# Expert tiles of 512 tokens, one written order for five engines, and a state product in two halves

## The chip, the cores and the metric

One core of a Trainium2 chip. The metric is the device time of the whole program in microseconds. The kernel before took 532.48 us (median of three runs, 531.59 to 532.96). One more execution was profiled; every duration below is from that one.

## What is computed

Three layers, one after the other, all in float32:

```python
# 1. gated linear attention, 4 x 8 heads, 768 positions, head size 32, state 16
y = (CB * L) @ x + (C @ state) * decay          # per chunk
state = decay_full * state + B^T @ (x * decay)
# 2. x: 3072 tokens x 256
h = x @ w_in                                    # 256 -> 2048
x = maximum(0.01 * h, h) @ w_out                # 2048 -> 256
# 3. one expert of 8 for each token
logits = x @ w_gate + modality_bias[modality_id]
e = argmax(logits, axis=1)
out[e == k] = gate_w * (maximum(x[e == k] @ w1[k], 0) @ w2[k])   # 256 -> 1024 -> 256
```

## The kernel before, in words

**Attention and the dense layer.** The 3072 tokens are 24 chunks of 128, six chunks to a batch, and six blocks of 512. A chunk's `p3_mm` (line 584) makes its output and the addition to the state; from the second chunk of a batch on it begins with the state product, one matmul of `st` (128 rows) with `cdt` (256 columns: the transposed decayed C twice, each masked to one half of the heads by `cdt_evict`, line 547, two ScalarE operations). Its PSUM tile `psy` is one bank of `psa`. `cb_mm` (line 559) multiplies in four row groups of 32, into four banks, two of them of `pscb`. The dense layer is float32 in three float32r products: each operand is a high part and a rest (high x high, high x rest, rest x high). For each of 96 steps (block j, f) `h_mm` (line 712) issues six matmuls of 512 columns and `mm2` (line 752) six more. VectorE and ScalarE make the activation's high part `gh` and rest `gl` in between (lines 724 to 745).

**Routing.** After each block the logits, the one-hot choice and the rank of each token in its expert's list are worked out (`logits`, `ranks`; lines 784 to 905); `ranks_put` (line 894) scatters the token numbers into the list `il` in DRAM with four indirect DMAs from GpSimd, and `rows_out` (line 926) writes the block's rows to `yx` in DRAM.

**Experts.** A tile is T = 256 entries of an expert's list. `m2_idx` (line 1010) reads the list (`gi`, which waits for all the scatters so far) and gathers the rows of `yx` by two indirect DMAs, `m2_w` (line 998) loads the expert's weights, `m2_split1` and `m2_split2` (lines 1028, 1037) split them into high part and rest (the last quarter on GpSimd, the others on VectorE), `m2_xT` (line 1043) transposes the rows, `m2_mm1` (line 1056) issues 48 matmuls of 256 columns into four PSUM tiles (`psh`, `pscb`), `m2_mm2` (line 1075) 48 more into one accumulator for each group of 128 tokens; then the result is scaled (ScalarE) and scattered (GpSimd). Five tiles are chosen by a table made after block 3 (`table_early`), seven more by a table made at the end (`table_final`); up to seven more stand in conditional code (`cond`, line 1258). 3072 tokens are twelve full tiles.

**What sets the order.** To the end of block 4, `PLAN` (line 26) is the written order of PE, VectorE, ScalarE and GpSimd: each token is a step and its numbers, and each engine executes its instructions in the order of the tokens (line 1182). Block 5 and the experts are scheduled by the framework, with some steps pinned (`Q["pin"]`, lines 1198 to 1255). There the first tile's first product is spread over block 5; at the block's end come the logits, the ranks, the second tile's first half, and the table. SyncE's queue (SP: loads, `gi`, `yx`) is ordered by the framework throughout.

Of the kernel before, what the change touches and what calls it, by code (L numbers as in the profile page):

```python
# [45 lines left out]
    mul.6.1 y.9 or.o.3.0 sa.12 lb.o.3.1 p3.6 gg.11 gh.10 or.o.3.1 gh.11 h.13 load.10 xa.6 cast.o.3.0 gl.10 trmm.7
    exp.7.1 st.6 trd.7 y.10 gg.12 subg.o.3.0 xb.6 trb.7 trde.7 trc.7 h.14 gl.11 gh.12 bs.7 sa.13 gl.12 exp.8.0 cb.7
    gg.13 y.11 mul.7.3 sa.14 mul.7.2 mul.7.0 exp.8.1 mul.7.1 mask.9 y.12 gg.14 gh.13 bt cast.o.3.1 h.15 gh.14 gl.13
    exp.9.1 p3.7 cd.8 subv.o.3.1 sa.15 gl.14 trmm.8 load.11 xa.7 trd.8 y.13 trb.8 gg.15 trde.8 trc.8 exp.9.0 xb.7 y.14
    cd.9 bs.8 st.7 gh.15 bs.9 gl.15 h.16 cb.8 sa.16 cd.10 mask.10 h.17 gg.16 mul.8.2 gh.16 mul.8.3 h.18 exp.10.0  # L50
    mul.8.1 mul.8.0 gl.16 sa.17 p3.8 sa.18 gg.17 exp.10.1 gg.18 trmm.9 load.12 y.15 st.8 trb.9 xa.8 trc.9 bs.10 trd.9
    evV.0 evA.0 h.19 trde.9 xb.8 gh.17 lg.0 sa.19 gl.17 y.16 lt.0 gg.19 l2.0 gh.18 h.20 r1.0 mask.11 r2.0 rx.0 cb.9
    sa.20 gl.18 exp.11.0 y.17 mul.9.0 mul.9.1 mul.9.2 exp.11.1 mul.9.3 rp.0 r3.0 trmm.10 be.0 trd.10 trb.10 y.18
    trde.10 gh.19 trc.10 put.0 gg.20 p3.9 gl.19 gh.20 cd.11 yr.0.0 st.9 xa.9 load.13 h.21 yc.0.0 xb.9 gl.20 bs.11
    yr.0.1 sa.21 y.19 yc.0.1 gg.21 mask.12 ro.0 cb.10 gh.21 exp.12.0 h.22 mul.10.3 mul.10.0 mul.10.2 exp.12.1 mul.10.1
    trmm.11 gl.21 p3.10 trc.11 sa.22 h.23 trb.11 load.14 gg.22 xa.10 xb.10 st.10 y.20 sa.23 bs.12 gg.23 h.24 gh.22
    gl.22 y.21 sa.24 gg.24 h.25 gh.23 gl.23 trd.11 sa.25 y.22 trde.11 gg.25 cb.11 cd.13 gh.24 mask.13 y.23 mul.11.1
    mul.11.3 exp.13.1 mul.11.2 mul.11.0 h.26 gl.24 gh.25 exp.13.0 gl.25 p3.11 sa.26 y.24 bs.13 load.15 xa.11 gg.26
    xb.11 h.27 gh.26 gl.26 y.25 cd.14 sa.27 mask.14 gg.27 h.28 gh.27 exp.14.0 gl.27 y.26 sa.28 exp.14.1 gg.28 y.27
    gh.28 h.29 gl.28 h.30 sa.29 gg.29 y.28 sa.30 gh.29 gg.30 h.31 gl.29 gh.30 gl.30 y.29 sa.31 gg.31 trmm.12 gh.31  # L60
    h.32 trc.12 mask.15 trb.12 gl.31 cb.12 sa.32 exp.15.0 y.30 gg.32 mul.12.2 mul.12.1 exp.15.1 h.33 mul.12.0 mul.12.3
    gh.32 p3.12 sa.33 gl.32 gg.33 trmm.13 xa.12 load.16 y.31 trc.13 trb.13 xb.12 st.12 bs.14 h.34 evV.1 evA.1 gh.33
# [98 lines left out]
def kernel(  # L161
# [1143 lines left out]
```

## Time and profile before

| | |
|---|---|
| median of three runs | 532.48 us |
| the profiled execution, its own time | 531.67 us |
| its span, first to last instruction | 530.0 us |
| mean granted clock of TensorE | 0.984 |
| PE / VectorE / ScalarE / GpSimd busy | 95% / 66% / 60% / 29% |

A PE row's own duration counts a matmul from issue to its drained result, so rows of successive matmuls overlap; what one costs is the distance to the next one's start, or a row of the chain of waits divided by its count. All helpers record through one line (L225), so groups are told apart by the names of their tiles: `h` and `y` are the dense layer's products, `hp` and `o` the experts' first and second, `psy`, `ps` and `cb` attention's, `lp`, `l`, `rp` and `yr` the routing's, `xps` the transposes of a tile's rows `xg`.

### The profile page before, as it was taken

To read this page: it belongs to the slowest core of one execution; us is meant where nothing else is said; L and a number is where in the kernel's file an instruction comes from. 1 tells how busy PE (TensorE), PEld (TensorE's weight loads), DVE (VectorE), ACT (ScalarE), POOL (GpSimd) and SP (SyncE) were. 2 spreads that over 40 slices of the span, in tenths; PEclk is the share of its full clock that TensorE was granted. 3 is DMA by queue.
4 is the path that set the end of the run, shared out by engine and by line. 5 is a ranking of instruction groups with operands and counts; after the bars stand their busy time and mean duration, and the time that the engine had idled before them with its cause. 6 is when DMAs were issued, how large, how long until landed. Compare 5 with 4: busy or idle time off the path is not lost.

```text
span 530.0 us, 9745 instructions
## 1 busy us (share of the span) xinstructions
PE 501.8 (95%) x3520; PEld 411.9 (78%) x3520; DVE 347.4 (66%) x737; ACT 317.4 (60%) x667; POOL 154.5 (29%) x143
## 2 busy tenths in 40 slices
PE   7879999999999999999999999999899999999990
PEld 4546767777876787778777787878799999999990
DVE  5898999775576656775677655674875555566620
ACT  5859989674764656456644544543566666666630
POOL 5343223040100310041011260220435655655340
PEclk8999999999999999999999999999999999999996
DMA  8899934529543251494001850090467777767300
GB/s 196 151 218 217 268 61 94 87 21 89 102 71 70 39 103 22 84 77 101 1 1 24 268 172 1 22 92 9 135 85 219 238 227 235 230 204 228 101 24 23
DMA packets 128315, 61.05 MB, mean 115 GB/s; under 512 B 84546, under 2 KB 120515, under 8 KB 128259
## 3 DMA queue, kind: packets, MB, share of 16 engines
q1 hardware_dynamic: 125186, 53.94, 48.1%
q0 software_dynamic: 3072, 6.41, 3.8%
q8 instruction: 30, 0.49, 0.5%
q14 instruction: 27, 0.21, 0.1%
HBM read 53.73 MB, written 6.60 MB: 114 GB/s over the span
## 4 chain that ended last, share of the span: by engine, by line
PE 78%; DVE 7%; ACT 6%; issue 4%; DMA 2%; POOL 1%; POOLq 0%; DVEq 0%; ACTq 0%
PE y L225 22%; PE h L225 22%; PE hp L225 12%; PE o L225 10%; PE psy L225 3%; PE cb L225 2%; DVE hb L225 2%; PE ps L225 1%; PE yr L225 1%; DMA raw<-in_moe_w_out_dram 1%; ACT e L225 1%; DVE gl L225 1%; PE xps L225 1%; PE lp L225 1%; ACT hb L225 1%
## 5 line engine op out<-in xcount | busy, mean ns | idle before, releaser
L225 ACT ACTIVATE sa<-h 128x512 f32<-128x512 f32 x96 | 56.8, 596 | 67.5 <-PE h L225 63.9
L225 DVE TENSOR_TENSOR gg<-sa,h 128x512 f32<-128x512 f32 x96 | 65.4, 684 | 46.8 <-ACT sa L225 46.1
L225 DVE TENSOR_TENSOR gl<-gg,gh 128x512 fp32r<-128x512 f32 x96 | 69.7, 728 | 23.4 <-ACT gh L225 22.0
L225 PE MATMUL h<-xh,wih 128*128 128x512 f32 x192 | 78.7, 410 | 1.9 <-DVE gg L225 1.7
L225 PE MATMUL y<-gh,woh 128*128 128x512 f32 x192 | 77.6, 413 | 0.0
L225 PE MATMUL y<-gl,woh 128*128 128x512 f32 x192 | 75.5, 393 | 0.8 <-DVE gl L225 0.8
L225 ACT CAST gh<-gg 128x512 fp32r<-128x512 f32 x96 | 59.3, 619 | 27.6 <-DVE gg L225 26.5
L225 PE MATMUL h<-xl,wih 128*128 128x512 f32 x192 | 75.3, 392 | 0.1
L225 PE MATMUL y<-gh,wol 128*128 128x512 f32 x192 | 75.3, 392 | 0.0
L225 PE MATMUL h<-xh,wil 128*128 128x512 f32 x192 | 75.3, 392 | 0.0
L225 PE MATMUL hp<-x2h,w1s 128*128 128x256 f32 x384 | 72.9, 286 | 0.0
L225 PE MATMUL o<-w2s,hh 128*128 128x256 f32 x384 | 69.3, 286 | 0.0
L225 DVE SCALAR_TENSOR_TENSOR hl<-hp,hh 128x512 fp32r<-128x512 f32 x48 | 33.0, 691 | 53.9 <-ACT hh L225 53.7
L225 PEld LDWEIGHTS hp<-x2h,w1s 128*128 128x128 f32 x384 | 62.1, 195 | 0.6
L225 PEld LDWEIGHTS o<-w2s,hh 128*128 128x128 f32 x384 | 58.4, 192 | 0.4 <-issue 0.4
L225 POOL DMA_INDIRECT il<-ids,pi x24 | 25.3, 1052 | 111.7 <-DVE base L225 79.8
L225 POOL TENSOR_SCALAR_AFFINE_SELECT e<-e 128x1024 f32<-128x1024 f32 (+1 forms) x28 | 28.7, 1031 | 97.8 <-DMA e<-cumd 69.3
L225 ACT ACTIVATE e<-e,ncum 128x128 f32<-128x128 f32 x160 | 50.8, 396 | 6.4 <-POOL e L225 6.4
L225 POOL TENSOR_TENSOR w2s<-r,w2s 128x1024 fp32r<-128x1024 f32 x12 | 33.4, 2785 | 71.5 <-ACT w2s L225 48.8
L225 PE MATMUL hp<-x2l,w1s 128*128 128x256 f32 x192 | 54.1, 287 | 0.0
L225 ACT ACTIVATE hh<-hp 128x512 fp32r<-128x512 f32 x48 | 28.5, 597 | 40.7 <-PE hp L225 40.7
L225 PE MATMUL o<-w2s,hl 128*128 128x256 f32 x192 | 51.1, 283 | 0.0
(195 smaller groups left out, 895.8 us busy)
## 6 DMA issues: line engine op xcount, KB each, us to landing
r<-in_moe_w_dram SPq DMA_DIRECT2D x48, 512.0 KB, 4.9
e<-cumd SPq DMA_DIRECT2D x20, 512.0 KB, 5.7
raw<-in_moe_w_in_dram SPq DMA_DIRECT2D x4, 1024.0 KB, 7.5
raw<-in_moe_w_out_dram SPq DMA_DIRECT2D x4, 1024.0 KB, 6.3
yx<-ysb SPq DMA_DIRECT2D x6, 528.0 KB, 12.7
xt<-in_x_dram SPq DMA_DIRECT2D x24, 128.0 KB, 4.7
ct<-in_C_dram SPq DMA_DIRECT2D x24, 64.0 KB, 4.5
bt<-in_B_dram SPq DMA_DIRECT2D x24, 64.0 KB, 4.0
```

Source lines behind the costliest of these rows:

```text
L225: r = f(*args, **kw)
```

## The change

- T is 512, so 3072 tokens are six full tiles: two from the early table, four from the final one, the rest conditional. A tile's first product (`m1`) is 8 x 6 matmuls of 512 columns in two PSUM tiles; its second (`m2`) goes step by step behind it, 12 matmuls of 256 columns for each f, into four accumulators at once (two banks of `psy` for even tiles, of `pscb` for odd ones). The last tile alone goes group by group (`m2q`).
- `PLAN` reaches to the end of the static tiles, is new from the middle of block 1 on, and orders SP too. In it: `w1`, `w2` load weights; `sh`, `sl` split them (`sl2.i.1` on GpSimd); `ix` reads `gi`; `ga` gathers (four DMAs of 128 rows); `xt` transposes, `xe` and `xf` evict; `re` and `rl` evict `m1`; `oe` scales; `sc` scatters; `tf1` to `tf4` make the final table. `put`, `ro`, `rp`, `be`, `yr`, `lg`, `l2`, `evA`, `evV` are the routing's steps as before, with the block's number.
- From chunk 4 on the state product is two matmuls of 64 rows and 128 columns, one for each half of the heads, into two banks; `cdt` is then one unmasked copy. The PSUM tile of `p3_mm` moves from `psa` to `pscb`, which is one buffer of two banks.

```diff
--- before
+++ after
@@ the order written out by hand: its end @@
+    sa.93 gg.93 h.94 gh.92 gl.92 y.91 sa.94 gg.94 xt.0 gh.93 gl.93 h.95 xe.0.0 xe.0.1 xf.0.0 y.92 sa.95 xf.0.1 sh1.1.0
+    gg.95 y.93 gh.94 sl1.1.0 sh1.1.1 m1.0.0 gl.94 gh.95 sl1.1.1 sh2.1.0 y.94 gl.95 sh2.1.1 xt.1 sl2.1.0 re.0.0 y.95
+    xe.1.1 rl.0.0 sl2.1.1 xe.1.0 xf.1.1 m1.0.1 evA.5 evV.5 xf.1.0 m1.0.2 re.0.1 rl.0.1 lg.5 re.0.2 rl.0.2 m1.0.3 lt.5
+    l2.5 re.0.3 yr.5.0 r1.5 m2.0.0 yc.5.0 r2.5 rx.5 r3.5 rp.5 rl.0.3 yr.5.1 be.5 m2.0.1 yc.5.1 ro.5 tf1 put.5 m2.0.2
+    tf2 m1.0.4 tf3 m1.0.5 re.0.4 tf4 m2.0.3 re.0.5 rl.0.4 w1.2 rl.0.5 m2.0.4 ix.2 w1.3 m1.0.6 ix.3 m1.0.7 re.0.6 ix.4
+    rl.0.6 ix.5 m2.0.5 re.0.7 ga.2 rl.0.7 m1.1.0 m1.1.1 re.1.0 rl.1.0 m2.0.6 re.1.1 w2.2 sh1.2.0 rl.1.1 m2.0.7 sh1.2.1
+    sl1.2.0 m2.1.0 oe.0.2 sl1.2.1 oe.0.0 oe.0.1 sc.0.0 m1.1.2 oe.0.3 w2.3 ga.3 xt.2 re.1.2 rl.1.2 m1.1.3 xe.2.1 xe.2.0
+    xf.2.1 m1.1.4 re.1.3 xf.2.0 rl.1.3 sh2.2.0 m2.1.1 sc.0.1 re.1.4 sl2.2.0 m1.1.5 sh2.2.1 sc.0.2 rl.1.4 m2.1.2 re.1.5
+    sl2.2.1 rl.1.5 m1.1.6 m2.1.3 re.1.6 sc.0.3 rl.1.6 w1.4 m1.1.7 xt.3 re.1.7 sh1.3.0 rl.1.7 m2.1.4 sh1.3.1 sl1.3.0
+    m1.2.0 xe.3.0 sl1.3.1 xe.3.1 m2.1.5 re.2.0 xf.3.1 rl.2.0 m1.2.1 xf.3.0 m2.1.6 re.2.1 w2.4 rl.2.1 m2.1.7 m1.2.2
+    sh2.3.0 sh2.3.1 sl2.3.0 m2.2.0 re.2.2 sl2.3.1 m1.2.3 oe.1.0 rl.2.2 oe.1.2 oe.1.3 m1.2.4 oe.1.1 re.2.3 ga.4 w1.5
+    rl.2.3 m2.2.1 re.2.4 rl.2.4 m1.2.5 m2.2.2 re.2.5 rl.2.5 m2.2.3 sc.1.0 m1.2.6 sc.1.1 m1.2.7 re.2.6 sc.1.2 rl.2.6
...
+    rl.4.7 m2.4.4 re.5.0 rl.5.0 m1.5.1 m1.5.2 re.5.1 rl.5.1 m2.4.5 re.5.2 rl.5.2 m1.5.3 m1.5.4 re.5.3 rl.5.3 m2.4.6
+    re.5.4 rl.5.4 m1.5.5 m2.4.7 re.5.5 rl.5.5 m1.5.6 oe.4.1 oe.4.0 oe.4.2 sc.4.0 m1.5.7 re.5.6 oe.4.3 rl.5.6 sc.4.1
+    re.5.7 rl.5.7 sc.4.2 m2q.5.0 sc.4.3 m2q.5.1 oe.5.0 sc.5.0 m2q.5.2 oe.5.1 sc.5.1 m2q.5.3 oe.5.2 sc.5.2 oe.5.3
+    sc.5.3
...
-    T = 256
+    T = 512
     KMAX = NT // T
-    EARLY = 5
-    NFIN = KMAX + NE - 1 - EARLY
+    EARLY = 2
+    NFIN = KMAX + NE - 1
     NSTAT = KMAX - EARLY
...
-    pscb = ctx.enter_context(tc.tile_pool(name="pscb", bufs=2, space=PSUM))
+    pscb = ctx.enter_context(tc.tile_pool(name="pscb", bufs=1, space=PSUM))
...
-    def cdt_evict(d, src):
+    def cdt_evict(c, d, src):
         cdt = ap_.tile([P, 2, P], F32, tag="cdt", name="cdt", bufs=2)
+        if c >= NC0:
+            d["cdt"] = cdt[:, 0, :]
+            readers.append(s.copy(out=d["cdt"], in_=src))
+            return
...
-        for q, (pool, tag) in enumerate(two + ((pscb, "cb"), (pscb, "cb"))):
-            cb = pool.tile([P, 512], F32, tag=tag, name="cb")[:, 0:2 * P]
+        c2 = pscb.tile([P, 2, 512], F32, tag="cb", name="cb")
+        for q in range(4):
+            cb = c2[:, q - 2, 0:2 * P] if q >= 2 else two[q][0].tile([P, 512], F32, tag=two[q][1], name="cb")[:, 0:2 * P]
...
-        ps = psa.tile([P, 512], F32, tag="a", name="psy")
-        if cc > 0:
-            t_.matmul(ps[:, 0:2 * P], lhsT=st, rhs=d["cdt"].rearrange("p q i -> p (q i)"), start=True, stop=False)
+        if c < NC0:
+            ps = psa.tile([P, 512], F32, tag="a", name="psy")
+            yq = ps[:, 0:2 * P].rearrange("p (q i) -> p q i", q=2)
+            bx = ps[:, 2 * P:2 * P + 64]
+            if cc > 0:
+                t_.matmul(ps[:, 0:2 * P], lhsT=st, rhs=d["cdt"].rearrange("p q i -> p (q i)"), start=True, stop=False)
+        else:
+            ps = pscb.tile([P, 2, 512], F32, tag="cb", name="psy")
+            yq = ps[:, :, 0:P]
+            bx = ps[:, 0, 2 * P:2 * P + 64]
+            if cc > 0:
+                for q in range(2):
+                    rs = slice(64 * q, 64 * q + 64)
+                    t_.matmul(yq[:, q, :], lhsT=st[rs, :], rhs=d["cdt"][rs, :], start=True, stop=False)
         for q in (1, 0):
             for k in (3, 2, 1, 0):
                 h = 4 * q + k
-                t_.matmul(ps[32 * k:32 * k + 32, q * P:(q + 1) * P], lhsT=d["x"][:, h, :], rhs=e[:, h, :], start=(cc == 0), stop=(cc == 0 or q == 0))
+                last = cc == 0 or c >= NC0 or q == 0
+                t_.matmul(yq[32 * k:32 * k + 32, q, :], lhsT=d["x"][:, h, :], rhs=e[:, h, :], start=(cc == 0), stop=last)
...
+    def e_ix(i):
+        tab, k = tl[i]
         vi = nc.values_load(tab[:, 1, k:k + 1], engines=[ENG.SP], min_val=0, max_val=NE * NT - T, skip_runtime_bounds_check_because=WHY)
-        gi = sp.tile([P, 2], I32, tag="gi", name="gi", bufs=6)
+        gi = sp.tile([P, NQ], I32, tag="gi", name="gi", bufs=6)
...
+    def e_ga(i):
+        d = ex[i]
+        lim = blocks[-2][0] if i < EARLY else NT + 1
+        d["xg"] = late_pool("raw2").tile([P, NQ, YW], F32, tag="xg", name="xg")
+        for q in range(NQ):
...
+    def e_sl(i, t, k):
+        r, hi, lo = e_raw(i, t, k)
+        (g if t == 2 and k == 1 else v).tensor_tensor(out=lo, in0=r, in1=hi.bitcast(F32), op=ALU.subtract)
...
+    def e_xt(i):
+        d = ex[i]
+        d["xp"] = [pool.tile([P, T], F32, tag=tag, name="xps") for pool, tag in ((psm, "m"), (psa, "a"))]
...
+            for q in range(NQ):
+                t_.transpose(d["xp"][k][:, q * P:(q + 1) * P], d["xg"][:, q, k * P:(k + 1) * P], ident)
...
+    def e_m1(i, f):
+        d = ex[i]
+        d["hp", f] = psh.tile([P, T], F32, tag="h", name="hp")
...
+                t_.matmul(d["hp", f], lhsT=d[1][:, k, part, fs], rhs=xx[:, k, :], start=(n == 0), stop=(n == 5))
...
+    def e_bank(i, n):
+        if n:
+            c2 = pscb.tile([P, 2, 512], F32, tag="cb", name="o")
+            return [c2[:, k, :] for k in range(2)]
+        return [psy.tile([P, 512], F32, tag="y", name="o") for _ in range(2)]
...
+    def e_m2(i, f):
+        d = ex[i]
+        if f == 0:
+            banks = e_bank(i, i % 2)
+            for q in range(NQ):
+                d["o", q] = banks[q // 2][:, (q % 2) * DM:(q % 2 + 1) * DM]
+        for q in range(NQ):
+            e_mm(i, f, q, f == 0 and q % 2 == 0)
+
+    def e_m2q(i, q):
+        d = ex[i]
+        if q % 2 == 0:
+            banks = e_bank(i, q == 0)
+            for k in range(2):
+                d["o", q + k] = banks[k][:, 0:DM]
+        for f in range(NF2):
+            e_mm(i, f, q, f == 0)
...
-    with tc.manual_schedule(engines={ENG.PE, ENG.DVE, ENG.Activation, ENG.Pool}):
+    with tc.manual_schedule(engines={ENG.PE, ENG.DVE, ENG.Activation, ENG.Pool, ENG.SP}):
...
```

## Rows read from the trace of the kernel before

**Rows 1.** Windows: us, PE, PEld, DVE, ACT, POOL busy (x count), clock, DMA share, GB/s.
```profile
57.00:371.00 314.00, 310.74 (x1956) 239.49 (x1955) 216.36 (x501) 188.26 (x444) 57.16 (x50) 1.00 0.44 75
371.00:392.00 21.00, 18.45 (x152) 17.44 (x151) 16.21 (x50) 10.75 (x17) 9.53 (x7) 0.92 0.48 129
392.00:516.40 124.40, 124.33 (x1041) 124.12 (x1039) 69.25 (x82) 75.56 (x111) 63.46 (x45) 1.00 0.62 183
516.40:530.00 13.60, 0.00 (x0) 0.00 (x0) 0.00 (x0) 0.47 (x1) 1.40 (x2) 0.62 0.07 22
```

**Rows 2.** The chain of waits in order of time: start us, us, what.
```profile
243.00 2.72 PE y L225 x12
...
388.49 0.44 PE yr L225 x4
...
409.23 5.76 PE hp L225 x48
```

**Rows 3.** Groups of PE by form: count | busy us, mean ns of one.
```profile
L225 PE MATMUL hp<-x2h,w1s 128*128 128x256 f32 x384 | 72.9, 286 | 0.0
...
L225 PE MATMUL hp<-x2l,w1s 128*128 128x256 f32 x192 | 54.1, 287 | 0.0
```

**Rows 4.** Timeline of PE, one chunk's cb and p3: start us, duration, what.
```profile
205.35 0.71 PE L225 MATMUL cb<-cm,btt 32*128 32x256 f32 x8
205.99 0.50 PE L225 MATMUL y<-gh,woh 128*128 128x512 f32 x1
...
208.85 0.59 PE L225 MATMUL psy<-cdt,st 128*128 128x256 f32 x2
209.37 0.65 PE L225 MATMUL psy<-e,xt 128*32 128x128 f32 x16
```

**Rows 5.** Timeline of PE between block 5 and the second tile.
```profile
379.66 0.63 PE L225 MATMUL hp<-x2h,w1s 128*128 128x256 f32 x4
382.33 0.19 PE L225 MATMUL rp<-ohb,tris 128*128 128x32 bf16 x1 [2.04 <-DVE ohb L225]
...
383.20 1.11 PE L225 MATMUL yr<-ident,yt 128*128 128x128 f32 x4 [0.51 <-DVE x2l L225]
```

**Rows 6.** The window around it (columns as in rows 1).
```profile
380.00:390.00 10.00, 7.45 (x56) 7.16 (x55) 7.37 (x35) 3.07 (x7) 6.52 (x6) 0.83 0.58 195
```

**Rows 7.** Timeline of GpSimd: block 5's scatters into the list, first and last of four.
```profile
384.39 0.98 POOL L225 DMA_INDIRECT il<-ids,pi  x1 [1.47 <-DVE nt L225]
...
388.24 0.98 POOL L225 DMA_INDIRECT il<-ids,pi  x1 [0.30 <-issue]
```

**Rows 8.** DMA issues, median us to landing: all; at 270 to 282; at 338 to 346.
```profile
il<-ids,pi POOLq DMA_INDIRECT x24, 8.6
...
il<-ids,pi POOLq DMA_INDIRECT x4, 7.9
...
il<-ids,pi POOLq DMA_INDIRECT x4, 14.4
```

**Rows 9.** Timelines of SP and GpSimd: a tile's list read, its two gathers; gathers' landing.
```profile
410.68 0.37 SPq L1013 DMA_DIRECT2D gi<-il  x1
...
414.74 1.05 POOL L225 DMA_INDIRECT xg<-yx,gi  x1 [1.42 <-issue]
416.10 1.02 POOL L225 DMA_INDIRECT xg<-yx,gi  x1 [0.31 <-ACT x2h L225]
...
xg<-yx,gi POOLq DMA_INDIRECT x14, 3.2
```

**Rows 10.** Timelines of GpSimd and VectorE: GpSimd's subtractions beside VectorE's operations.
```profile
52.92 1.54 POOL L225 TENSOR_TENSOR wil<-hb,wih 128x512 fp32r<-128x512 f32 x1 [3.03 <-ACT wih L225]
53.23 1.28 DVE L225 TENSOR_TENSOR gg<-sa,h 128x512 f32<-128x512 f32 x2
...
345.20 3.58 DVE L225 TENSOR_TENSOR gl<-gg,gh 128x512 fp32r<-128x512 f32 x1 [0.24 <-ACT gh L225]
345.82 2.40 POOL L225 TENSOR_TENSOR w2s<-r,w2s 128x1024 fp32r<-128x1024 f32 x1
```

More of the change, by code (lines that the diff above doesn't have):

```diff
@@ L46 @@
[L46 to L50, printed above, removed]
@@ L602, in p3_mm @@
                 )
-        d["psy"] = ps
+        d["yq"], d["bx"] = yq, bx
     def p3_x(c):
@@ L1018, in m2_idx @@
             )
-        lim = blocks[-2][0] if tab is tabe else NT + 1
-        xg = late["raw2"].tile([P, 2, YW], F32, tag="xg", name="xg", bufs=6)
-        for q in range(2):
+        ex.setdefault(i, {})["gi"] = gi
+    def e_ga(i):
[3 more added lines that the diff above has]
+        for q in range(NQ):
             g.indirect_dma_start(
-                out=xg[:, q, :], out_offset=None, in_=yx[0:lim, :],
-                in_offset=IndirectOffsetOnAxis(ap=gi[:, q:q + 1], axis=0), bounds_check=lim - 1, oob_is_err=False,
-            )
@@ L1075, in m2_mm2 @@
-    def m2_mm2(i):
-        d = m2.pop(i)
-        for q in range(2):
-            qs = slice(q * P, (q + 1) * P)
-            o = psy.tile([P, 512], F32, tag="y", name="o")[:, 0:DM]
-            for f in range(NF2):
-                hh, hl = d["h"][f // 2]
-                for n, (h, part) in enumerate(((hh, 0), (hh, 1), (hl, 0))):
-                    t_.matmul(o, lhsT=h[:, f % 2, qs], rhs=d["w2"][:, f, part, :], start=(f == 0 and n == 0), stop=(f == NF2 - 1 and n == 2))
-            gate = d["xg"][:, q, DM:DM + 1]
-            o2 = late["raw2"].tile([P, DM], F32, tag="o2", name="o2")
-            s.activation(out=o2, in_=o, func=AF.Copy, scale=gate)
-            w = g.indirect_dma_start(
-                out=out, out_offset=IndirectOffsetOnAxis(ap=d["gi"][:, q:q + 1], axis=0),
-                in_=o2, in_offset=None, bounds_check=NT - 1, oob_is_err=False,
-            )
-            tc.declare_no_dep(w.ins, group="out", reason="the rows that two scatters write are disjoint")
-            tc.add_to_no_dep_group("out", w.ins)
+                out=d["xg"][:, q, :], out_offset=None, in_=yx[0:lim, :],
@@ new lines, in e_h, with e_re, e_rl @@
+    def e_h(i, f, hl):
+        d = ex[i]
+        if i != KMAX - 1:
+            d[hl, f] = gp.tile([P, T], F32R, tag="g", name=hl)
+        else:
+            if hl not in d:
+                d[hl] = late_pool("wp2").tile([P, NF2, T], F32R, tag="w", name=hl)
+            d[hl, f] = d[hl][:, f, :]
+        return d[hl, f]
+    def e_re(i, f):
+        s.activation(out=e_h(i, f, "hh"), in_=ex[i]["hp", f], func=AF.Relu)
+    def e_rl(i, f):
+        d = ex[i]
+        v.scalar_tensor_tensor(
+            out=e_h(i, f, "hl"), in0=d["hp", f], scalar=0.0, in1=d["hh", f].bitcast(F32), op0=ALU.max, op1=ALU.subtract
+        )
@@ new lines, in e_oe, with e_sc @@
+    def e_oe(i, q):
+        d = ex[i]
+        d["o2", q] = late_pool("raw2").tile([P, DM], F32, tag="o2", name="o2", bufs=4)
+        s.activation(out=d["o2", q], in_=d["o", q], func=AF.Copy, scale=d["xg"][:, q, DM:DM + 1])
+    def e_sc(i, q):
+        d = ex[i]
+        w = g.indirect_dma_start(
+            out=out, out_offset=IndirectOffsetOnAxis(ap=d["gi"][:, q:q + 1], axis=0),
+            in_=d["o2", q], in_offset=None, bounds_check=NT - 1, oob_is_err=False,
+        )
+        tc.declare_no_dep(w.ins, group="out", reason="the rows that two scatters write are disjoint")
+        tc.add_to_no_dep_group("out", w.ins)
```

423 lines of the change are left out of this document (153 added, 270 removed).

## The prediction, made before the change was built

> **What bounds the kernel now.** I read the windows first: the time in stretches, and in each the engine that has no room. From 57 to 371 us PE is busy 310.7 of 314 us, from 392 to 516.4 us 124.3 of 124.4 [rows 1]; no other engine passes 70% there. So PE's own work sets the time, and a change gains only by making PE's work shorter or by closing PE's few gaps. There are three outside the first 57 us: 3.3 us spread over the long stretch, 2.55 us in the stretch between block 5 and the second expert tile, and the last 13.6 us, in which the result of the last matmul is scaled, scattered and the program ends [rows 1]. A busy PE is still not a PE at its rate, so next I took its rate from the chain of waits: 12 matmuls of 512 columns take 2.72 us, 227 ns each; 48 of 256 columns take 5.76 us, 120 ns each [rows 2]. Two short ones cost 240 ns where a long one costs 227.
>
> **Part 1, wider tiles.** The first product has 384 + 192 = 576 matmuls of 256 columns [rows 3], which is 12 tiles of 48: the static tiles all ran and the conditional ones did not, so each expert's count is a multiple of 256, and I take six full tiles of 512 for the change. They become 288 of 512 columns: 576 x 0.120 = 69.1 us go, 288 x 0.227 = 65.3 us come. **Minus 3.8 us**, all on PE. The second product keeps its 576 matmuls of 256 columns, transposes and gathers and scatters keep their number (each moves 128 tokens): zero. Weight loads and splits halve, from twelve to six; VectorE, ScalarE and GpSimd have room in that stretch [rows 1], so this too is worth zero. The last tile ends by groups as before, so the 13.6 us of the tail stay.
>
> **Part 2, evictions beside GpSimd.** The second product now follows the first step by step, so a quarter of the next tile's weights is subtracted on GpSimd while VectorE evicts `hp`. Such a subtraction stopped a VectorE operation that reads only SBUF: `gl` took 3.58 us around a GpSimd operation of 2.40 [rows 10]. But two `gg`, which read PSUM, went through in 1.28 us beside GpSimd's 1.54 [rows 10], and `rl`, `xf` and the evictions of `y` read PSUM too. I take zero; without that cover a tile would lose up to 2.4 us, which belongs to the upper end.
>
> **Part 3, the state product.** 17 chunks from chunk 4 on are not the first of their batch. Today `psy<-cdt,st` stands 0.52 us ahead of the next product [rows 4]: two passes of 256 columns and a change to another layout of the array. `cb`, four row groups side by side, needs 0.64 us for the same two passes of 256 columns [rows 4], although its eight instructions in series would need about four times 0.43: row groups do run together, and a change of layout in and out costs some 0.2 together, 0.1 each (an estimate from these two rows). Halves of 128 columns side by side save one pass's length, 0.21, and enter one more layout, 0.1: 0.1 for each chunk, **minus 1.8 us**. Ends: 0.21 x 17 = 3.6 us less if the entry is free, 1.8 us more if the halves run one after the other. I take the middle because `cb` is the nearest row and shows both effects. The Trainium skill's TensorEngine Tiling (Array Packing), Key Properties, says that tiles work independently but that switching the mode drains the engine; its table gives two row tiles up to a factor of two. By the table alone this part would be worth the 3.6 us; the drain speaks against it, and the 0.2 us that `cb` pays beyond its two passes agrees with the drain.
>
> The masked copies that go (17 ScalarE operations) and the move of `psy` to `pscb` I cost at nothing: ScalarE is busy 188 of 314 us [rows 1], and the same readers free the bank that the next `cb` waits for. If that cover failed, a chunk would wait for one eviction.
>
> **Part 4, the written order in blocks 1 to 4.** It can close at most the 3.3 us of gaps [rows 1] and can open as many. Zero, with plus or minus 2 for the range. SP's queue in written order has nothing urgent there.
>
> **Part 5, between block 5 and the experts.** Before, PE ran out after four `hp` at 379.66 and got the ranks at 382.33 [rows 5], because the one-hot was late on VectorE; in the ten microseconds around it PE is idle 2.55 us and the granted clock averages 0.83 [rows 6], that is 0.17 x 2 x 10 = 3.4 us on the lower of its two levels, half of it lost: 1.7 us. Together 4.3. The new order puts `m1.0.1` and `m1.0.2` ahead of `lg.5`, `m1.0.3` ahead of `l2.5`, `m2.0.0` ahead of `rp.5`; each is 1.36 or 1.44 us of PE work against chains of a few short operations. I keep 0.3 us: **minus 4.0 us**.
>
> **Part 6, the wait that is added.** The third tile is the first from the final table. Its rows need, in this order: block 5's ranks, four scatters into the list, the list read, four gathers; and PE, in written order, stops at `xt.2` until the last of them has landed. From the rows:
> - `rp` at 382.33 to the first scatter at 384.39: 2.1 us [rows 5, 7];
> - first to last scatter: 3.85 [rows 7];
> - the last scatter's landing: 8.6, the median of all 24; four of one block had 7.9, four others 14.4 [rows 8];
> - the list read, issue on SP to the first gather on GpSimd: 4.1 [rows 9], and some 0.3 for SP to wake;
> - three more gathers at 1.36, 4.1; the last lands 3.2 after its issue [rows 9].
>
> That is 26.2 us from `rp.5` to the moment `xt.2` can end. Between them PE has in the written order `yr.5.1` (0.4), seven `m1` at 1.36 (9.5) and eight `m2` at 1.44 (11.5), by the rates of [rows 2]: 21.4 us. PE stands still for 26.2 - 21.4 = **plus 4.8 us**. Behind `xt.2` on PE are the rest of tile 1 and all else; SP holds `w1.3` to `w2.2` behind the list read, GpSimd holds `sc.0.0`, `ga.3` and `sl2.2.1` behind the gathers, and all of those are needed only 10 us later. The wait is longer than the one at 380, which was followed by 3.4 us at the lower clock level [rows 6], so I add **1.7 us** again. The ends: 7.9 for the landing gives 4.1 us, 14.4 gives 10.6.
>
> **Sum.** -3.8 - 1.8 - 4.0 + 4.8 + 1.7 = -3.1. The profiled execution took 531.67 us (span 530.0), the median is 532.48; so 528.6 against the first, and **529.4 us** against the median, which is what I give. A measurement of this kernel can tell about 0.3%, 1.6 us, from no change.
>
> **Rivals.**
> 1. *The list is there in time.* The Trainium skill's DMA: Bandwidth & Descriptors, Latency and other measured facts, puts the fixed cost of a DMA at about 2 us; the scatters here took 7.9 to 14.4 [rows 8]. If the landing were short (under 3.8 us, so that 26.2 falls to 21.4) parts 1, 3 and 5 stand alone: -9.6, 522.9 us. For it: gathers and plain loads land in about 3 us [rows 9], and the scatters' landing might be counted late. Against it: 24 of them say 8.6. Chance 0.25.
> 2. *Slower: the list is later still.* Same place, but with the landing of block 4, 14.4 us, since the new order writes the block's rows (`ro.5`) just ahead of the scatters. PE stands 10.6 us and loses 1.7 to the clock: +12.3 - 9.6 = +2.7, 535.2 us. It decides from a landing of about 12 us on. Chance 0.16.
> 3. *The halves do not run side by side,* or the new order loses in the middle what they gain: part 3 turns to +1.8, and the sum to +0.5, 533.0 us, no difference. For it: the drain. Against it: `cb`. Chance 0.09.
> 4. The forecast: 0.5, with a range of its own of 527 to 532.
>
> **How the numbers follow.** Faster by over 0.3%: all of the first rival (0.25) and four fifths of the forecast (0.40), 0.02 from the third: 0.67. Within 0.3%: the rest of the forecast (0.10) and most of the third rival (0.07): 0.17. Slower: 0.16. The range goes from 521, the first rival with part of the state product's upper end, to 535.5, which takes in the second.
>
> **What would show it.** Right: in the profile after, `hp` has 288 matmuls of 512 columns and 2.72 us for 12; PE has one long gap ended by the DMA of `xg`, some 100 us ahead of the last matmul, with a lower granted clock behind it, and no other gap over 1 us in the expert stretch; the window between block 5 and tile 0 is full; the state product to the next product takes about 0.42 us. Wrong: no gap at `xt.2` (rival 1), one over 8 us (rival 2), a state product of 0.5 us or more (rival 3), or gaps of PE inside the expert tiles that end with VectorE, which would undo part 2.

## The result, and the profile after

The changed kernel takes **535.61 us** (median of five runs, 535.29 to 536.71) against 532.48 for the kernel before: ratio 1.0061, 95% interval 1.0043 to 1.0079. It is slower, by 3.1 us, where 529.4 was forecast; it lies 0.1 us above the range. The profiled execution took 535.73 us with a span of 533.9; before it was 531.67 and 530.0, so the two spans differ by 3.9 us, and that is the sum to be explained.

The windows of the changed kernel, with the columns of [rows 1]:

```profile
57.00:371.00 314.00, 311.52 (x1981) 239.63 (x1982) 227.79 (x511) 190.34 (x439) 59.30 (x50) 1.00 0.42 71
371.00:392.00 21.00, 21.00 (x152) 18.38 (x151) 11.87 (x48) 5.50 (x11) 3.92 (x4) 1.00 0.46 41
392.00:400.00 8.00, 6.93 (x48) 6.13 (x46) 3.83 (x4) 4.84 (x9) 0.66 (x1) 1.00 0.94 237
400.00:410.00 10.00, 2.06 (x6) 1.21 (x7) 0.69 (x1) 0.36 (x1) 7.69 (x8) 0.63 0.97 298
410.00:420.00 10.00, 10.00 (x53) 8.70 (x52) 4.50 (x6) 4.64 (x7) 6.44 (x5) 0.86 0.21 60
420.00:521.00 101.00, 101.00 (x667) 92.56 (x665) 37.31 (x49) 42.10 (x71) 35.33 (x30) 1.00 0.24 79
```

The second line answers to the second of [rows 1]: PE is busy all 21 us at the full clock where it had 18.45 and 0.92. So the gap between block 5 and the experts is closed. The sixth line shows the expert tiles without a gap. All that PE loses late stands in one place, 399 to 410 us, with a clock of 0.63 in that window and 0.86 in the next. PE's waits between 371 and 521 us are one line, and the timeline of PE there shows what it waits for (columns as in [rows 5]):

```profile
PE xps L1006 <- DMA xg<-yx,gi: 9.0, 4, 5.1
```

```profile
398.54 0.39 PE L1025 MATMUL hp<-x2h,w1s 128*128 128x512 f32 x1
403.99 0.45 PE L1006 MATMUL xps<-ident,xg 128*128 128x128 f32 x1 [5.07 <-DMA xg<-yx,gi]
406.77 0.48 PE L1006 MATMUL xps<-ident,xg 128*128 128x128 f32 x1 [2.33 <-DMA xg<-yx,gi]
...
409.34 1.33 PE L1006 MATMUL xps<-ident,xg 128*128 128x128 f32 x5 [0.71 <-DMA xg<-yx,gi]
410.32 0.78 PE L1025 MATMUL hp<-x2h,w1s 128*128 128x512 f32 x1
```

Each of the four gathers is met by a wait of PE. The wait is where the prediction put it, at the third tile's transposes, and is twice as long. The timelines of GpSimd and SP give the chain ahead of it: first and last scatter, the list read, first and last gather, and the loads `r` of expert weights around them (eight transfers of 512 KB, issued from 383.97 to 401.70).

```profile
379.29 0.99 POOL L835 DMA_INDIRECT il<-ids,pi  x1 [8.35 <-DVE cm L919]
383.15 0.98 POOL L835 DMA_INDIRECT il<-ids,pi  x1 [0.31 <-issue]
...
399.34 1.25 POOL L977 DMA_INDIRECT xg<-yx,gi  x1 [15.21 <-DMA gi<-il]
403.53 1.00 POOL L977 DMA_INDIRECT xg<-yx,gi  x1 [0.30 <-issue]
```

```profile
383.97 0.90 SPq L948 DMA_DIRECT2D r<-in_moe_w_dram  x2
392.36 0.38 SPq L964 DMA_DIRECT2D gi<-il  x1
393.26 0.86 SPq L948 DMA_DIRECT2D r<-in_moe_w_dram  x2
...
396.99 5.08 SPq L955 DMA_DIRECT2D r<-in_moe_w_dram  x4
```

The DMA issues with their median time to landing, at 383.5 to 385, 392 to 397 and 399 to 404 us:

```profile
r<-in_moe_w_dram SPq DMA_DIRECT2D x2, 512.0 KB, 12.4
...
gi<-il SPq DMA_DIRECT2D x4, 2.0 KB, 6.2
...
xg<-yx,gi POOLq DMA_INDIRECT x4, 5.8
```

Gathers land in 5.8 us where they had 3.2 before [rows 9]. From the last scatter to the list read it takes 9.2 us, about what [rows 8] had as the median, 8.6, and not the 14.4 of block 4.

Then the other end of the program. These are the first and the 528th of `y`'s 576 matmuls (the 528th is in the middle of block 5, ahead of any product of an expert), in the timeline of PE, first of the kernel before, then of the changed one:

```profile
44.37 0.39 PE L225 MATMUL y<-gh,woh 128*128 128x512 f32 x1
...
345.41 0.39 PE L225 MATMUL y<-gh,wol 128*128 128x512 f32 x1
```

```profile
46.13 0.39 PE L695 MATMUL y<-gh,woh 128*128 128x512 f32 x1
...
347.49 0.39 PE L695 MATMUL y<-gh,wol 128*128 128x512 f32 x1
```

The changed kernel is 1.76 us late at the first, ahead of any step whose order on the four compute engines was changed, and 2.08 late at the 528th, although its state products are shorter by then. (These are one execution of each; how much of it is the kernel's is asked below.) Two of these in the same timeline, and the first product's groups, answer to [rows 4] and [rows 3]:

```profile
211.10 0.49 PE L547 MATMUL psy<-cdt,st 64*128 64x128 f32 x4
211.52 0.64 PE L552 MATMUL psy<-e,xt 128*32 128x128 f32 x16
```

```profile
L1025 PE MATMUL hp<-x2h,w1s 128*128 128x512 f32 x192 | 66.1, 398 | 0.0
...
L1025 PE MATMUL hp<-x2l,w1s 128*128 128x512 f32 x96 | 38.2, 398 | 0.0
```

The state product takes 0.42 us to the next one where it took 0.52, and `hp` is 288 matmuls of 512 columns.

### The profile page after: what moved, and what is told of

Its sections match the earlier page's. It is cut to its first block, busy times and chain, and to the rows that moved or that the text cites. A ratio compares the mean times of both kernels' runs of the same rounds, so it can differ in the third digit from the quotient of the medians.

```text
span 533.9 us, 8921 instructions
## 1 busy us (share of the span) xinstructions
PE 499.9 (94%) x3266; PEld 396.9 (74%) x3266; DVE 331.3 (62%) x719; ACT 288.1 (54%) x626; POOL 138.3 (26%) x137
## 3 DMA queue, kind: packets, MB, share of 16 engines
q0 software_dynamic: 3072, 6.41, 3.8%
## 4 chain that ended last, share of the span: by engine, by line
PE 62%; issue 13%; DMA 8%; POOL 5%; DVE 5%; ACT 4%; SPq 1%; POOLq 0%; ACTq 0%; DVEq 0%
PE h L655 24%; PE y L695 23%; POOL out_dram L1086 3%; PE hp L1025 3%; PE cb L512 2%; PE o L1056 2%; PE psy L552 2%; DMA xg<-yx,gi 2%; DMA il<-ids,pi 2%; DMA gi<-il 1%; PE psy L547 1%; DVE gl L677 1%; PE yr L852 1%; DMA e<-cumd 1%; DMA il<-sent 1%
## 5 line engine op out<-in xcount | busy, mean ns | idle before, releaser
L677 DVE TENSOR_TENSOR gl<-gg,gh 128x512 fp32r<-128x512 f32 x96 | 75.2, 787 | 14.6 <-ACT gh L672 13.0
L695 PE MATMUL y<-gh,woh 128*128 128x512 f32 x192 | 78.7, 410 | 0.0
L1025 PE MATMUL hp<-x2h,w1s 128*128 128x512 f32 x192 | 66.1, 398 | 0.0
L1056 PEld LDWEIGHTS o<-w2s,hh 128*128 128x128 f32 x384 | 61.2, 190 | 2.2
L1056 PE MATMUL o<-w2s,hl 128*128 128x256 f32 x192 | 54.1, 282 | 0.0
L655 PEld LDWEIGHTS h<-xh,wih 128*128 128x128 f32 x192 | 36.0, 188 | 15.5 <-DVE gg L667 4.1
L399 POOL TENSOR_SCALAR_AFFINE_SELECT e<-e 128x1024 f32<-128x1024 f32 x20 | 25.0, 1256 | 79.0 <-DMA e<-cumd 45.4
L695 PEld LDWEIGHTS y<-gh,woh 128*128 128x128 f32 x192 | 36.1, 188 | 10.8 <-issue 3.1
L1025 PEld LDWEIGHTS hp<-x2h,w1s 128*128 128x128 f32 x192 | 36.8, 192 | 7.4 <-issue 0.2
```

The costliest lines, as they stand in the source:

```text
L399: g.affine_select(out=e, in_=e, pattern=[[0, H], [1, P]], compare_op=ALU.is_ge, fill=NEG, base=0, channel_multiplier=-1)
L655: t_.matmul(h, lhsT=w[:, k, fs], rhs=xx[:, k, :], start=(i == 0), stop=(i == 5))
L677: v.tensor_tensor(out=gl, in0=d["gg"], in1=d["gh"].bitcast(F32), op=ALU.subtract)
L695: t_.matmul(y_t[j][k], lhsT=w[:, f, ds], rhs=gg, start=(f == 0 and i == 0), stop=(f == NF - 1 and i == 2))
L1025: t_.matmul(d["hp", f], lhsT=d[1][:, k, part, fs], rhs=xx[:, k, :], start=(n == 0), stop=(n == 5))
L1056: t_.matmul(d["o", q], lhsT=d[h, f][:, q * P:(q + 1) * P], rhs=d[2][:, f, part, :], start=(start and n == 0), stop=(f == NF2 - 1 and n == ...
```

## The experiments

Two theories came out of this: the third tile's rows are late because their list read and gathers run beside the weight loads; and the first 60 us lose time because SP is now held in the written order. All ratios are to the kernel before, run beside them; the change itself has 1.0061.

### Is the whole loss the wait at the third tile?

```diff
- w2.3 ga.3 xt.2 re.1.2 rl.1.2 m1.1.3 xe.2.1 xe.2.0 xf.2.1 m1.1.4 re.1.3 xf.2.0
- m1.1.7 xt.3 ... m2.1.4 ... m1.2.0 xe.3.0 ... xe.3.1 m2.1.5 ... m1.2.1
+ w2.3 ga.3 re.1.2 rl.1.2 m1.1.3 m1.1.4 re.1.3
+ m1.1.7 ... xt.2 xe.2.1 xe.2.0 xf.2.1 xf.2.0 m2.1.4 ... m2.1.5 m1.2.0 ... xt.3 xe.3.0 ... m1.2.1
```

> Edit: the third tile's transposes and their four evictions move in the written order from ahead of m1.1.3 to ahead of m2.1.4, with m2.1.5 ahead of m1.2.0 and the fourth tile's transposes behind m1.2.0; nothing is left out. Theory (the whole loss is PE standing at these transposes): five more first-product steps and three second-product steps, 5 x 1.36 + 3 x 1.44 = 11.1 us, lie ahead of the wait that now costs PE 9.0 us idle and about 2.5 us of slower matmuls behind it; the wait ended by xg falls below 1 us and the time to 524 us (523 to 526). Rival (the stall only moves: the later weights or the fourth tile's rows are late next): PE stands elsewhere in the same 30 us for 3 us or more, 527 to 532 us.

Measured: 524.17 us, ratio 0.9861 (0.9839 to 0.9883). PE's only wait between 371 and 510 us, and the window in which the change stands still:

```profile
PE hp L1026 <- DVE hl L1044: 1.1, 1, 1.1
```

```profile
392.00:416.00 24.00, 22.89 (x152) 20.61 (x151) 11.99 (x14) 12.46 (x20) 14.00 (x12) 1.00 0.80 225
```

The wait is gone, only 1.1 us have taken its place, and the clock stays full. From the 528th `y` to the last matmul's end the changed kernel takes 521.05 - 347.49 = 173.6 us, this one 509.60 - 346.60 = 163.0: **the wait with its lower clock costs 10.6 us**. The theory holds, and the version is faster than both kernels. Run once more, beside runs that stand further below:

> The version with the third tile's transposes late, unedited, as the measure for the other three of this group. All theories: its ratio to the kernel before as it was, 0.986 (0.983 to 0.989).

524.95 us, 0.9856 (0.9827 to 0.9884): as before.

### Why are the rows late?

The four weight loads of the change's third and fourth tile (eight transfers, 4 MB) are held until the rows have landed; the splits of the third tile's weights move behind them.

```diff
- w1.2 ... ix.2 w1.3 ... ix.3 ... ix.4 ix.5 ... ga.2 ... w2.2 ... w2.3
+ ix.2 ... ix.3 ... ix.4 ix.5 ... ga.2 w1.2 w2.2 w1.3 w2.3
+            if i == EARLY:
+                tc.add_manual_dep(r.ins, ex[i]["last"].name, ...
```

> Edit: the third tile's transposes stay where the change has them; the weight loads w1.2, w2.2, w1.3, w2.3 (4 MB) are held until the last of the third tile's four gathers has landed, and the splits of the third tile's weights move behind m1.1.5 and m1.1.7. Theory (the list read and the gathers are slow because they share the DMA engines with these loads): the list read, issue to first gather, falls from 7.0 us to about 4.1 and the last gather's landing from 5.8 to about 3.2, as rows of the kernel before have them; PE's wait falls from 9.0 to about 4 us and the time by 5 us to 530.5 us (529 to 532). Rival (the loads do not matter; the landing of the scatters or the list's 4-byte elements make it late): the wait stays at 9 us, 535 to 537 us, or more if the weights are then late.

Measured: 528.35 us, 0.9932 (0.9907 to 0.9957). PE's wait, GpSimd's last scatter, first and last gather, and the landings of list reads and gathers:

```profile
PE xps L1012 <- DMA xg<-yx,gi: 2.3, 3, 1.0
```

```profile
384.31 0.98 POOL L836 DMA_INDIRECT il<-ids,pi  x1 [0.30 <-issue]
396.28 1.05 POOL L983 DMA_INDIRECT xg<-yx,gi  x1 [10.99 <-DMA gi<-il]
...
400.27 1.01 POOL L983 DMA_INDIRECT xg<-yx,gi  x1 [0.30 <-issue]
```

```profile
gi<-il SPq DMA_DIRECT2D x4, 2.0 KB, 3.4
xg<-yx,gi POOLq DMA_INDIRECT x4, 2.8
```

List reads land in 3.4 us instead of 6.2, gathers in 2.8 instead of 5.8; the theory holds. The wait fell further than expected, to 2.3 instead of 4, because the scatters' landing came 1.4 us earlier too. Two more runs split the loads: in the first all four stand behind the list reads but are not held (its edit is shown), in the second the first stays ahead of the list read (`w1.2 ix.2`) and three are held.

```diff
- w1.2 ... ix.2 w1.3 ... ix.3 ... ix.4 ix.5 ... ga.2 ... w2.2 ... w2.3
+ ix.2 ... ix.3 ... ix.4 ix.5 w1.2 w2.2 w1.3 w2.3 ... ga.2
```

> Edit against the change: the four weight loads w1.2, w2.2, w1.3, w2.3 stand in SP's order behind the four list reads instead of around them, and are held by nothing else; the splits of the third tile's weights move as in the run with weights last. Theory A (the first load, issued ahead of the list read, is what makes the list late): the list read, issue to first gather, takes 4.2 us instead of 7.0 and the last scatter's wait 7.8 instead of 9.1, but the gathers still land in about 5.8 beside the loads; PE's wait falls from 9.0 to about 5 us and the ratio to the kernel before from 1.006 to about 0.998 (0.995 to 1.001). Theory B (the loads beside the gathers are what counts): the wait stays at 8 us or more, ratio 1.003 to 1.007.

> Edit against the change: the first weight load w1.2 stays ahead of the list read, the other three are held until the last of the third tile's gathers has landed; splits as in the run with weights last. Theory A: the list read keeps 6 to 7 us behind the first load, the gathers land in 2.8; PE's wait falls from 9.0 to about 6 us, ratio 1.000 (0.997 to 1.003). Theory B: list read about 4, gathers 2.8, wait 2 to 3 us, ratio 0.993 as with all four held.

Measured: 531.55 us, 0.9977 (0.9950 to 1.0003), and 533.99 us, 1.0028 (0.9996 to 1.0060). By time the two overlap, and the second overlaps the change's 1.0061 (1.0043 to 1.0079) too; what tells them apart is the chain. PE's wait in the one and in the other:

```profile
PE xps L1007 <- DMA xg<-yx,gi: 5.3, 3, 4.0
```

```profile
PE xps L1012 <- DMA xg<-yx,gi: 5.6, 4, 3.0
```

The chain from the same timelines, one execution each, in us:

| | predicted | change | all held | behind the list | first early |
|---|---|---|---|---|---|
| first to last scatter | 3.85 | 3.9 | 3.9 | 3.9 | 3.9 |
| last scatter to list read | 8.9 | 9.2 | 7.8 | 7.7 | 9.6 |
| list read to first gather | 4.1 | 7.0 | 4.2 | 4.5 | 6.3 |
| first to last gather | 4.1 | 4.2 | 4.0 | 4.0 | 4.0 |
| last gather's landing | 3.2 | 5.8 | 2.8 | 6.0 | 2.8 |
| PE's wait | 4.8 | 9.0 | 2.3 | 5.3 | 5.6 |

In the chains Theory A holds in both. The loads slow what runs beside them: the first costs the scatters' landing and the list read some 4 us, the others cost the gathers 3 us. The Trainium skill's DMA: Bandwidth & Descriptors, Issuing engines are not separate DMA queues, says that transfers started by different engines run on the same 16 DMA engines and interleave; the rows agree, 5.8 us for a gather from GpSimd's queue beside SP's loads and 2.8 without them.

### Where do the first 347 us lose time?

SP is left out of the written order up to block 0's eviction.

```diff
-    with tc.manual_schedule(engines={ENG.PE, ENG.DVE, ENG.Activation, ENG.Pool, ENG.SP}):
-        for token in PLAN.split():
+    for part, engines in (
+        (steps[:cut], {ENG.PE, ENG.DVE, ENG.Activation, ENG.Pool}),
+        (steps[cut:], {ENG.PE, ENG.DVE, ENG.Activation, ENG.Pool, ENG.SP}),
+    ):
```

> Edit: the written order holds PE, VectorE, ScalarE and GpSimd as in the change, but the SP queue only from block 0's eviction on; ahead of that SP's transfers are ordered as the kernel before had them ordered, by the scheduler. The matmuls of blocks 0 to 3 end 2.1 us later in the change's trace than before although its state products are 1.7 us shorter, so 3.8 us are lost there, 1.8 of them already at the first product of y. Theory A (the SP queue's written order costs them in the first 60 us): the first y comes 1.8 us earlier, 533.5 to 534 us. Theory B (the order of the steps on the compute engines costs them): no difference, 535.6 us.

Measured: 533.42 us, 1.0039 (1.0026 to 1.0052). That is 1.2 us under the change by the ratios, and the two intervals overlap. In the traces the first `y` is back at its place, and the 528th comes 2.05 us ahead of the change's:

```profile
44.35 0.39 PE L695 MATMUL y<-gh,woh 128*128 128x512 f32 x1
```

It would be natural to look for a load that comes late: with the queue free three loads of `e` leave together from 31.55 us on, in written order the third of them stands behind a load of `x` and leaves at 42.81. But the same kernel run again (below) sends it at 43.50 and has its first `y` at 45.15, ahead of 46.13. The traces show two other things. The first of chunk 0's output products, in the kernel before, in the change, and in the change run again:

```profile
19.46 0.65 PE L225 MATMUL psy<-e,xt 128*32 128x128 f32 x16
```

```profile
20.46 0.64 PE L552 MATMUL psy<-e,xt 128*32 128x128 f32 x16
```

```profile
19.46 0.64 PE L552 MATMUL psy<-e,xt 128*32 128x128 f32 x16
```

So 1.00 of the 1.76 us is there at 20 us, and a second profile of the same kernel doesn't have it: eight products of `bc` ahead of it take 1.59 us in the change's trace and 1.06 in the two others. A first product later than 19.5 us stands in eight of the eleven profiles with the queue bound and in none of the five with it free; whether the order has a part in it, and what makes those matmuls slow, no run shows. From this product to the first `y` the kernel before takes 24.91 us, the change 25.67, the free queue 24.89. These 0.76 us are a wait of PE for `xl`, which only the change of the three has:

```profile
PE h L655 <- DVE xl L576: 0.9, 1, 0.9
```

Behind it stand a load of `e`, GpSimd's mask of it and VectorE's `hb`, the operation ahead of `xl`; first in the change, then with the queue free:

```profile
29.87 0.53 SPq L394 DMA_DIRECT2D e<-cumd  x1
...
37.16 1.54 POOL L399 TENSOR_SCALAR_AFFINE_SELECT e<-e 128x1024 f32<-128x1024 f32 x1
...
37.79 1.46 DVE L606 SCALAR_TENSOR_TENSOR hb<-raw,hb 128x512 int32<-128x512 int32 x1
```

```profile
31.55 3.61 SPq L394 DMA_DIRECT2D e<-cumd  x3
...
36.77 0.69 DVE L606 SCALAR_TENSOR_TENSOR hb<-raw,hb 128x512 int32<-128x512 int32 x1
...
37.29 1.13 POOL L399 TENSOR_SCALAR_AFFINE_SELECT e<-e 128x1024 f32<-128x1024 f32 x1 [1.10 <-DMA e<-cumd]
```

In written order the first load of `e` leaves *early*. GpSimd then masks `e` without a wait, beside `hb`, and both take longer: 1.54 and 1.46 us instead of 1.13 and 0.69. With the queue free the mask waits for its data until `hb` is almost done. The sixteen profiles fall into two kinds by this: with `hb` at 1.46 us it is 25.6 to 25.7 us from that first product to the first `y`, with 0.69 it is 24.9. All eleven with the queue bound are of the first kind. Of the five with it free four are of the second; the fifth (late rows with the queue free, run again) sends its first load of `e` at 30.85, masks at 35.87 and has 1.46. So it is the meeting of the two operations that costs 0.8 us, and the queue's order decides most often whether they meet. The reverse, the kernel before with SP added to its written order:

```diff
-    with tc.manual_schedule(engines={ENG.PE, ENG.DVE, ENG.Activation, ENG.Pool}):
+    with tc.manual_schedule(engines={ENG.PE, ENG.DVE, ENG.Activation, ENG.Pool, ENG.SP}):
```

> Edit: the kernel before, with SP added to the engines of its written order (blocks 0 to 4, in its own order of steps); nothing of the change besides. Theory (to hold SP's queue in the written order costs the first 60 us some 2 us): 1.5 to 2.5 us slower than the kernel before. Rival (it was only this plan's place for the transfers): no difference to the kernel before.

Measured: 1.0064 (1.0040 to 1.0088), 3.4 us slower by the ratio: slower for certain, and by more than the theory's 1.5 to 2.5. In PE's timeline

```profile
46.17 0.39 PE L225 MATMUL y<-gh,woh 128*128 128x512 f32 x1
```

the same 1.8 us at the first `y`, made of the same two parts: 1.01 at the first product (20.47), and a `hb` of 1.46. What the rest of the 3.4 us is was not taken apart. The first `y` by itself doesn't tell the two orders apart: it comes at 44.4 to 46.3 us in the profiles with the queue bound, at 44.1 to 44.9 in those with it free. To the steps' order on the other engines, two runs: the steps of the kernel before up to late in block 3, then the change's, with SP bound and with SP free.

```diff
- PLAN of the change up to y.63
+ PLAN of the kernel before up to y.63
```

> Edit: the steps up to block 3's last but two products are issued in the written order of the kernel before, the rest in that of the change; SP stays in written order. Theory B (the new order of the steps costs the 3.8 us, or the 2 of them behind the first y): 532 to 534 us. Theory A (SP's order costs them): no difference, 535.6 us.

> Edit against the change: the steps up to block 3's last but two products in the order of the kernel before, and the SP queue free up to there, so that of the change's first 330 us only the state product in halves and its place in the banks of cb remain; the third tile's transposes stand early, as in the change. The kernel before has the end of block 4's y products but one block at 345.4 us. Theory C (the new order of the steps costs the other 1.7 us that the free queue doesn't give back): that point comes at 343.7 us, and the time is 3.8 us under the change, 531.8 us. Theory D (sharing one pair of banks between cb and the state product costs them): 345.4 us, and 533.5 us as with the free queue alone.

Measured: 539.94 us, 1.0178 (1.0136 to 1.0219), and 536.95 us, 1.0077 (1.0048 to 1.0106), with the 528th `y` at 347.94 us. None of the theories had this. The old order of steps is worse for the changed kernel: from first to 528th `y` it needs 304.7 us with SP bound and 303.8 with SP free, where the new order needs 301.4 and 301.1 (and 300.2 to 302.9 in six more profiles of the same steps). Against the kernel before, at 301.0, the last run keeps only the halves and their place in the banks of `cb`, and loses 2.8 us where the halves should have given 1.7; so the old steps and the new state product in its banks do not go together, and the new steps are better than the old ones there. Whether the halves or the banks do it was not tried. In the change's own profile the new steps need 0.3 us more than the kernel before, where the halves should make it 1.7 less: 2.0 us lost. With 2.7 us between profiles of the same steps, and one profile of the kernel before, how much of that is order, banks or scatter stays open.

### The state product

> The change itself, unedited, as the measure for the other three of this group. All theories: as it was, 535.6 us (534.5 to 536.7), PE's wait for xg at the third tile's transposes 9.0 us.

> Edit: from chunk 4 on the state product goes back to two matmuls over all 128 rows with the two masked copies, in the banks that the change gives it; all else as in the change. Theory (a product in halves is worth the 0.10 us a chunk that the traces show, 0.52 to 0.42, and all of it is on the path): 17 x 0.10 = 1.7 us slower than the change, 537.3 us. Rival (a shorter state product is lost again in waits for its copies): no difference, 535.6 us.

Measured: 538.19 us, 1.0095 (1.0062 to 1.0128), for the change, above its expected 535.6, and 1.0116 (1.0068 to 1.0165) with the whole state: not told apart. The kernel before spreads over 5.6 us beside these runs, where it spreads over 4.1 and 3.7 in the groups ahead and behind. So the question was put again, on the version with late rows:

```diff
-                    t_.matmul(yq[:, q, :], lhsT=st[rs, :], rhs=d["cdt"][rs, :], start=True, stop=False)
+                    t_.matmul(yq[:, q, :], lhsT=st, rhs=d["cdt"][:, q, :], start=True, stop=False)
```

> Edit against the version with late rows: from chunk 4 on the state product over all 128 rows in two matmuls with its two masked copies. The profile of the first such run has 0.54 us from it to the next product, where the change has 0.42. Theory (17 x 0.12 on the path): 2.0 us slower than late rows. Rival (lost in other waits): equal.

Measured: 526.92 us, 0.9904 (0.9873 to 0.9935), against 0.9856 (0.9827 to 0.9884) in the same group: 2.0 us by the medians, with intervals that just touch. The timeline of PE in one chunk:

```profile
211.48 0.60 PE L543 MATMUL psy<-cdt,st 128*128 128x128 f32 x4
212.01 0.64 PE L548 MATMUL psy<-e,xt 128*32 128x128 f32 x16
```

0.53 us to the next product instead of 0.42; the theory's 2 us agree with the medians, and the rows show the place.

### Both losses mended

Late rows and the free queue together, run twice:

> Edit: the late transposes of the third tile (as in the run with late rows) and the SP queue free up to block 0's eviction (as in the run with the queue free), together. Theory (two separate losses): 524.2 less 2.1, so 522 us (521 to 523.5), faster than both kernels. Rival (the earlier start only makes the third tile's rows late again, or the gain of the free queue was a matter of one run's start): 524 us.

> Edit against the version with late rows: the SP queue free up to block 0's eviction. In the first run of this pair of edits the profile showed some 6 us lost between 210 and 300 us that the version with the queue alone free doesn't show. Theory (those are that chip's late transfers, and the queue is worth 2 us): 2 us, 0.4%, faster than late rows in this group. Rival (in this version the free queue costs the middle what it saves at the start): equal to late rows or slower.

Measured: 529.89 us, 0.9916 (0.9889 to 0.9944); then **523.01 us, 0.9821 (0.9793 to 0.9849)**, beside late rows alone at 524.95, 0.9856 (0.9827 to 0.9884). The first series missed both its cases. All its nine times (527.4 to 532.9) lie above all six of the second (521.2 to 524.4), and from first to 528th `y` its profile needs 306.8 us, the second's 300.2, with the same instructions. It ran on another chip than the second, the same as the change run again, whose ratio was higher there too (1.0095 for 1.0061); what makes the middle longer was not found. In the second series the 528th `y` is 1.3 us ahead of late rows alone, but that lead is all there at the first output product (19.18 against 20.47), and this is the profile with the queue free and a `hb` of 1.46. So that the free queue adds to the late rows is not shown: the two intervals overlap, and the profile doesn't bear it out. That this version beats both kernels is shown twice.

## Why the prediction was wrong

By its own steps, from the profiled executions (spans 530.0 and 533.9):

| step | predicted | measured |
|---|---|---|
| wider tiles, evictions, gap before the experts | -7.8 | -7.9 |
| state product in halves | -1.8 | -1.7 |
| start, and written order in blocks 0 to 4 | 0 | +3.8 |
| the wait for the third tile, with the clock | +6.5 | +10.6 |
| tail | 0 | -0.8 |
| sum | -3.1 | +4.0 |

**Parts 1, 2 and 5: right in their sum.** From the 528th `y` to the last matmul the kernel before takes 516.33 - 345.41 = 170.9 us, the version with late rows 163.0: 7.9 us less. No eviction waits for GpSimd (101.00 of 101 us busy), and the gap at block 5 is closed. Part 1 alone is smaller than forecast, because its rate was read from `y`: 12 of the new `hp` take 2.79 us (row below), not 2.72, so 288 take 67.0 and not 65.3 us, and the gain is 2.1 instead of 3.8. The rest of the 7.9 then came by more than part 5's 4.0; where was not taken apart, so that the sum agrees to 0.1 is in part luck.

**Part 3: right**, in size and in its choice of the middle: 17 x (0.42 - 0.52) = -1.7, and 2.0 us by the medians of the last test. The Trainium skill's TensorEngine Tiling (Array Packing), Key Properties, has a switch of mode drain the engine; that 0.10 us was saved of the 0.21 that a pass of the other half takes is in line with it; no run takes the switch itself apart.

**Part 4: wrong.** The step that failed is "Zero, with plus or minus 2", and in it "SP's queue in written order has nothing urgent there". The +3.8 of the profiles has three parts. 1.0 us is there at the first output product, and the same kernel run again doesn't have it; its cause is open. 0.8 us is `hb` beside GpSimd's mask, in the first 57 us, which the prediction set aside. It is not that something urgent came late: a load came early, and its mask met a VectorE operation. That meeting has a price in the prediction's own [rows 10] (`gl` 3.58 us around a GpSimd operation), which part 2 asked about in the experts alone. The last 2.0 us are 301.35 - 301.04 = 0.3 more from first to 528th `y`, where the halves should have made it 1.7 less; that is within the scatter of the profiles. That something is lost there the times do show, by an estimate: without the wait the change should be 7.9 + 1.7 + 0.8 = 10.4 us faster than the kernel before, and by the ratios late rows is 7.4 and 7.7. Of these some 3 us the 0.8 has its cause shown, and the rest stays open.

**Part 6: mechanism right, size wrong.** The place, the waiting tile and the gap's 111 us from the last matmul came as written. Of the chain's terms the scatters and their landing came out, at 9.2 for 8.9. The mis-sized ones are "the list read, issue on SP to the first gather on GpSimd: 4.1" (7.0) and "the last lands 3.2 after its issue" (5.8): 5.5 us of the chain, and the table of the four runs gives both back, each when its own loads are moved. Both prices were read in [rows 9], where weights were coming in too, but two transfers at a time. These two landed at 416.92 and 418.15, beside the gathers of 414.74 and 416.10:

```profile
412.08 0.92 SPq L1002 DMA_DIRECT2D r<-in_moe_w_dram  x2
```

The change issues eight around its chain. The prediction itself said that SP holds `w1.3` to `w2.2` behind the list read, and looked only at who needs them, not at what they do to the gathers that run beside them. The first load, ahead of the list read, was not looked at. The clock's 1.7 was near: 12 matmuls of 512 columns after the wait took 3.82 us (granted clock 0.86 from 410 to 420 us), against 2.79 for 12 at full clock, and the transposes 0.5 more.

```profile
370.15 2.79 PE hp L1025 x12
...
410.67 3.82 PE hp L1025 x12
```

(Two pieces of the chain of waits.) **The second rival** gave 535.2 us and the time is 535.6, but its mechanism did not happen: the landing of the scatters was 9.1 us and not 14.4. Its sign, a gap over 8 us, did happen (9.0), so the sign could not tell it from a longer list read. A time can agree for another reason; the chain's own rows decide. By the table, either failed step alone would have left the time inside the range and within 0.3% of before; it took both. In the first rival, that "plain loads land in about 3 us [rows 9]" is a wrong reading: those rows have gathers alone, and the medians of plain loads in that trace are 4.0 us and more.

## What to carry to other kernels

Price a transfer with what the new order starts beside it: a gather's 3 us, taken beside two transfers of weights, became 6 under four weight loads, and those loads were in the written order to be read. A DMA queue put into written order moves the times at which data arrive, earlier ones too, and with them which operations of GpSimd and VectorE meet; compare arrivals, not only waits. And before a difference of one or two us between two traces is put down to an edit, profile the same kernel again: here 1.0 us of it was gone in the second profile. Where a chain is late, moving its reader ten microseconds of other work later can be worth more than making the chain fast: here 2.0% of the time against 1.3% for holding the loads.

## What was not expected of the hardware

The first weight load, two transfers of 512 KB issued 0.8 us behind the last scatter, landed after 12.4 us. The windows from 384 to 392 us, of the changed kernel and of the run with all loads held:

```profile
384.00:392.00 8.00, 8.00 (x52) 7.15 (x51) 2.09 (x4) 1.34 (x4) 0.13 (x1) 1.00 1.00 36
```

```profile
384.00:392.00 8.00, 8.00 (x54) 7.27 (x53) 3.22 (x9) 1.79 (x3) 0.99 (x2) 1.00 0.03 2
```

With the load beside the scatters the DMA engines show a busy share of 1.00 and move 36 GB/s; with the scatters alone it is 0.03, and the scatters still need 7.6 us to land. So four scatters of 128 numbers neither fill the engines nor land soon, and a large load issued behind them hardly moves. The busy share is no measure of what moves: single packets of 4 KB of that load last up to 7.9 us. In the run with all loads held the scatters' own packets are over at 386.1 us, 1.8 us behind the last issue, and from there to the landing at 391.9 the trace has no packet of data at all. The Trainium skill's DMA: Bandwidth & Descriptors, Latency and other measured facts, puts a DMA's fixed cost at about 2 us; the gathers alone, at 2.8, come near it, the scatters do not. What the scatters wait for in those 5.8 us was not tried.
